# A linear-attention block with a GEGLU layer: regrouping the k^T v products, W_q's fold and the warming products

## The chip, the cores and the metric

The kernel runs on one core of a Trainium2 chip. The metric is the device time of one execution in microseconds (us); lower is better. Five engines work at once, each through its own list of instructions in order: TensorE (PE; its weight loads are shown apart as PEld) multiplies matrices and writes into PSUM, VectorE (DVE), ScalarE (ACT) and GpSimd (POOL) do elementwise work, and SyncE (SP) issues most DMA transfers. Semaphores make an instruction wait for another engine.

## What is computed

The input x has 2048 rows of 640. Attention has 32 heads of 20 columns, the feed-forward layer 1536 columns.

```python
def _A_ref(x, wqkv, w_phi, wo):          # H = 32, Dh = 20
    q, k, v = split(x @ wqkv)            # each [H, S, Dh]
    pq = einsum("bhsd,hdf->bhsf", q, w_phi)
    pk = einsum("bhsd,hdf->bhsf", k, w_phi)
    phi_q = concatenate([softmax(pq), softmax(-pq)], axis=-1)
    phi_k = concatenate([softmax(pk), softmax(-pk)], axis=-1)
    kv = einsum("bhsf,bhsd->bhfd", phi_k, v)
    z  = einsum("bhsf->bhf", phi_k)
    num = einsum("bhqf,bhfd->bhqd", phi_q, kv)
    den = einsum("bhqf,bhf->bhq", phi_q, z)[..., None] + 1e-6
    return merge_heads(num / den) @ wo
def _B_ref(x, w_gate, w_up, w_down):
    return (gelu(x @ w_gate) * (x @ w_up)) @ w_down
h = x + _A_ref(layernorm(x), wqkv, w_phi, wo)
return h + _B_ref(layernorm(h), w_gate, w_up, w_down)
```

The sum kv (and z) runs over all 2048 rows, so no row's attention can be finished before the last row's k and v are in it.

## The kernel before

The 2048 rows are 16 tiles of 128 rows (t = 0 to 15), four tiles to a block b. The 640 columns are five chunks of 128. The order of instructions on every engine is written out by hand: each engine runs its instructions in the order in which the program emits them.

PSUM has eight banks. Until the feed-forward part is well under way they are four buffers of two banks each (pool psG, tag "G"), which every matmul group takes in turn: a group waits until the engine that reads the buffer's former content is done.

**Opening (L187 to L230, L439 to L489).** SyncE issues the loads of x and of W_v, then transposing loads of W_k. TensorE meanwhile multiplies ones by ones (`warm`, L226 to L230; the result is never read): two products of 512 columns and 28 of 128, and four more of 128 at L447. The first real work are transposes of the first two tiles (L164) and the v products of tiles 0 to 2 (L312).

**Folding (`fold`, L232 to L259).** The per-head matrices w_phi are multiplied into W_k and W_q, so that one product with x gives pk or pq. For each of five row blocks d, TensorE multiplies the transposed weights by a block-diagonal matrix of w_phi (BD); the result wa fills two PSUM banks and is copied to bf16. Heads of 20 columns don't divide chunks of 128, so `runs` lists the pieces (bank, part, chunk, first and last column). W_k is folded with two parts of 320 columns, six products a block; W_q with `quarters` true in four parts of 160 columns, eight products a block, and the copy (L254 to L257, all on ScalarE) reorders the columns so that each 32-column piece of a head quarter lies in its place. W_q's folds run at t = 10 to 14 (L504).

**The loop over tiles (L494 to L534).** For each t: k's products (`k_tile`, L331) and exponentials, v's products for t + 3, softmax sums and normalization (`k_norm`, L343; VectorE and GpSimd). kv accumulates in one PSUM buffer kvp that stays taken from t = 3 on. `kv_tile` (L368) adds one row tile: 32 products of 32 x 40 outputs, four of them on different quarters of the array. They are issued in bursts: tiles 0 to 3 at t = 9 and 4 to 8 at t = 13 (`KVG`), tiles 9 to 12 at t = 15 behind the second group of q products (`KVQ`, L57 and L512), and tiles 13 to 15 behind the loop (L539).

**q (`q_mm`, `q_exp`, L387 to L401).** `QG` lists which (block, chunk) pairs form a group; a group has one or two, each of five products of 512 columns. Groups 0 to 3 run at t = 15; q = 4 is the first group behind the loop. After the exponentials of group 2 a one-element copy by GpSimd (L536) releases the load of W_gate.

**Attention's first tiles (L831 to L882).** `kv_mask` (L377) on VectorE scales kvp into KT and transposes it into KV. `attn_a` multiplies 40 small products (L585, tile ab) and copies them out; `attn_b`, `b2` and `b3` divide; `attn_t` transposes o; `attn_c` multiplies by W_o (L707). TensorE fills the time with the remaining q groups. Nine of the ten products of group q are issued ahead of `attn_a(0, 1)`, the tenth behind it (L831 to L834); `q_exp(q)` comes behind.

**The rest.** Gate and up products (L767), the down product (L789) and the attention of the remaining tiles are woven together by `weave`.

## Time and profile before

| | us |
|---|---|
| median of three runs | 271.77 |
| lowest and highest of them | 271.55, 272.08 |
| the profiled execution | 271.61 |
| its span, first to last instruction | 269.9 |

| engine | busy us |
|---|---|
| TensorE, products | 265.8 |
| TensorE, weight loads | 171.4 |
| VectorE | 174.9 |
| ScalarE | 138.9 |
| GpSimd | 101.0 |

The profile is taken from one execution. A row of a timeline has the start in us from the span's first instruction, the length, the engine, the line, the operation, what is written and read, its shape and how many were merged; in brackets stands how long the engine was idle before and what ended the idle time. A row of the chain has start, length and what the end of the kernel waited for at that moment. A matmul's recorded length includes its way through the array, so rows of neighbouring groups overlap; the chain cuts them where the next begins to count.

### The profile page before, as it was taken

To read this page: it belongs to the slowest core of one execution; us is meant where nothing else is said; L and a number is where in the kernel's file an instruction comes from. 1 tells how busy PE (TensorE), PEld (TensorE's weight loads), DVE (VectorE), ACT (ScalarE), POOL (GpSimd) and SP (SyncE) were. 2 spreads that over 40 slices of the span, in tenths; PEclk is the share of its full clock that TensorE was granted. 3 is DMA by queue.
4 is the path that set the end of the run, shared out by engine and by line. 5 is a ranking of instruction groups with operands and counts; after the bars stand their busy time and mean duration, and the time that the engine had idled before them with its cause. 6 is when DMAs were issued, how large, how long until landed. Compare 5 with 4: busy or idle time off the path is not lost.

```text
span 269.9 us, 7043 instructions
## 1 busy us (share of the span) xinstructions
PE 265.8 (98%) x2867; PEld 171.4 (64%) x2867; DVE 174.9 (65%) x347; ACT 138.9 (51%) x249; POOL 101.0 (37%) x238
## 2 busy tenths in 40 slices
PE   8999999999999999999999999999999999999995
PEld 6777777755456887788755555775555476444574
DVE  6889999997876858875576783568664322333322
ACT  5789998877789665245541456321554400322100
POOL 5548988796002335375211664014661100000000
PEclk9999999999999999999999999999999999999999
DMA  7989389310688343332202222203222101000011
GB/s 195 227 193 168 66 208 94 59 27 2 236 275 249 122 101 70 33 98 51 53 23 51 49 50 51 51 0 84 75 41 49 24 24 51 24 0 0 4 49 49
DMA packets 45264, 22.10 MB, mean 82 GB/s; under 512 B 37808, under 2 KB 43184, under 8 KB 45232
## 3 DMA queue, kind: packets, MB, share of 16 engines
q1 hardware_dynamic: 44576, 21.64, 33.6%
q8 instruction: 22, 0.36, 0.5%
q10 hardware_dynamic: 656, 0.03, 0.2%
q14 instruction: 10, 0.08, 0.1%
HBM read 10.18 MB, written 2.62 MB: 47 GB/s over the span
## 4 chain that ended last, share of the span: by engine, by line
PE 97%; DMA 2%; SPq 0%; DVE 0%; issue 0%
PE gu L767 39%; PE pd L789 20%; PE pq L396 8%; PE pk L296 8%; PE po L707 8%; PE pv L296 7%; PE kvp L374 2%; PE pv L312 2%; DMA Wv<-in_A_wqkv_dram 2%; PE ab L618 1%; PE wa L248 1%; PE ab L585 1%; PE tp L164 0%; SPq L193 0%; SPq L190 0%; SPq L189 0%
## 5 line engine op out<-in xcount | busy, mean ns | idle before, releaser
L770 ACT ACTIVATE g<-gu 128x512 bf16<-128x512 f32 (+1 forms) x60 | 30.4, 510 | 73.8 <-PE gu L767 73.0
L773 DVE TENSOR_TENSOR GT<-gu,g 128x512 bf16<-128x512 f32 (+1 forms) x60 | 34.4, 580 | 47.1 <-PE gu L767 39.2
L767 PE MATMUL gu<-LN2T,Wg 128*128 128x512 bf16 (+1 forms) x300 | 61.8, 337 | 0.0
L767 PE MATMUL gu<-LN2T,Wu 128*128 128x512 bf16 (+1 forms) x300 | 61.7, 336 | 0.0
L789 PE MATMUL pd<-Wd,GT 128*128 128x320 bf16 (+4 forms) x396 | 53.9, 295 | 0.0
L789 PEld LDWEIGHTS <-GT 128*128 128x128 bf16 x396 | 37.6, 98 | 14.5 <-DVE GT L773 0.2
L767 PEld LDWEIGHTS <-Wu 128*128 128x128 bf16 x300 | 29.3, 98 | 22.6
L767 PEld LDWEIGHTS <-Wg 128*128 128x128 bf16 x300 | 29.0, 98 | 21.2
L296 PEld LDWEIGHTS <-LN1T 128*128 128x128 bf16 x290 | 27.9, 98 | 10.5
L355 POOL TENSOR_TENSOR E<-E,rs 128x640 bf16<-128x640 bf16 x25 | 31.6, 1296 | 4.4 <-DVE rs L351 4.1
L791 DVE TENSOR_TENSOR y<-pd,x_sb 128x320 bf16<-128x320 f32 (+4 forms) x33 | 15.8, 480 | 23.8 <-PE pd L789 23.8
L707 PE MATMUL po<-Wo,oT 128*128 128x320 bf16 x160 | 24.5, 299 | 0.0
L296 PE MATMUL pk<-Wk,LN1T 128*128 128x320 bf16 x160 | 24.4, 299 | 0.0
L396 PE MATMUL pq<-LN1T,Wq 128*128 128x512 bf16 x100 | 22.9, 379 | 0.0
L347 DVE TENSOR_REDUCE sk<-E 128x64 f32<-128x1280 bf16 x16 | 22.9, 1430 | 0.0
L401 ACT ACTIVATE Eq<-pq 128x1024 bf16<-128x1024 f32 (+1 forms) x26 | 19.9, 831 | 2.8 <-PE pq L396 2.7
L340 ACT ACTIVATE E<-pk 128x640 bf16<-128x640 f32 x28 | 18.8, 747 | 3.0 <-PE pk L296 3.0
L707 PEld LDWEIGHTS <-oT 128*128 128x128 bf16 x160 | 15.6, 98 | 7.3 <-ACT oT L165 0.2
L296 PE MATMUL pv<-Wv,LN1T 128*128 128x320 bf16 x130 | 19.8, 299 | 0.0
L151 ACT ACTIVATE ln<-x_sb,v,rstd 128x640 bf16<-128x640 bf16 x14 | 12.9, 920 | 13.3 <-POOL v L746 13.2
L396 PEld LDWEIGHTS <-Wq 128*128 128x128 bf16 x100 | 9.4, 98 | 10.3
L682 DVE TENSOR_TENSOR tt<-AB,w 128x1280 bf16<-128x1280 f32 x10 | 15.1, 1506 | 0.4 <-POOL w L675 0.3
(120 smaller groups left out, 290.6 us busy)
## 6 DMA issues: line engine op xcount, KB each, us to landing
out_dram<-y SPq DMA_DIRECT2D x15, 160.0 KB, 1.8
x_sb<-in_A_x_dram SPq DMA_DIRECT2D x6, 320.0 KB, 3.4
Wu<-in_B_w_up_dram SPq DMA_DIRECT2D x1, 1920.0 KB, 8.9
Wg<-in_B_w_gate_dram SPq DMA_DIRECT2D x2, 768.0 KB, 5.6
Wd<-in_B_w_down_dram SPq DMA_DIRECT2D x1, 1440.0 KB, 6.7
Wo<-in_A_wo_dram SPq DMA_DIRECT2D x1, 800.0 KB, 5.1
x_sb<-in_A_x_dram SPq DMA_DIRECT2D x4, 160.0 KB, 2.8
Wv<-in_A_wqkv_dram SPq DMA_DIRECT2D x2, 320.0 KB, 4.3
```

The source lines that it names most:

```text
L296: nc.tensor.matmul(ps[:, u, 0:HD], lhsT=lnT(t, c), rhs=W[:, c, u * HD:(u + 1) * HD], start=(c == 0), stop=(c == NC - 1))
L340: nc.scalar.activation(Ek[t][:, s, :].rearrange("p (u f) -> p u f", u=2), pk[:, :, 0:HD], ACTF.Exp, scale=((lnp[t][2], nrstd[t]) if t in C ...
L347: nc.vector.reduce_sum(sk, Ek[t].rearrange("p s (h f) -> p (s h) f", f=Dh), axis=AX.X)
L355: eng.tensor_tensor(e, e, rs[:, s * H:(s + 1) * H, None].to_broadcast([P, H, Dh]), ALU.mult)
L396: nc.tensor.matmul(pqs[j][:, i, :], lhsT=Wq2[:, kc, c * P:(c + 1) * P], rhs=LN1T[b][:, kc, :], start=(kc == 0), stop=(kc == NC - 1))
L401: nc.scalar.activation(Eq[j][:, :, s, :], pqs[j][:, 0:len(QG[j])], ACTF.Exp, scale=(1.0, -1.0)[s])
L707: nc.tensor.matmul(pos[u], lhsT=st[t][:, c, :], rhs=Wo[:, c, u * HD:(u + 1) * HD], start=(c == 0), stop=(c == NC - 1))
L767: nc.tensor.matmul(gu[i][:, 0:n], lhsT=W[:, c, f * P:(f + 1) * P], rhs=LN2T[b][:, c, a0:a1], start=(c == 0), stop=(c == NC - 1))
L770: nc.scalar.activation(g[:, 0:n], gu[0][:, 0:n], ACTF.Gelu_apprx_tanh)
L773: nc.vector.tensor_tensor(st[b, "g", f][:, a0:a1], gu[1][:, 0:n], g[:, 0:n], ALU.mult)
L789: nc.tensor.matmul(pd[:, 0:f1 - f0], lhsT=st[b, "g", f][:, tl * P:(tl + 1) * P], rhs=Wd[:, f, f0:f1], start=(f == 0), stop=(f == NF - 1), ...
L791: nc.vector.tensor_tensor(y[:, f0:f1], pd[:, 0:f1 - f0], x_sb[b][:, tl, f0:f1], ALU.add)
```

## The change

```diff
@@ -54,7 +54,6 @@
     KVG = {9: (0, 1, 2, 3), 13: (4, 5, 6, 7, 8)}
-    KVQ = {1: (9, 10, 11, 12)}
     VC = Dh + 1
@@ -227,12 +226,12 @@
-    warm(*[512] * 2, *[P] * 28)
+    warm(*[512] * 8, *[P] * 4)
 
     def fold(WT, W2, quarters, ds=range(NC)):
 
 
-        n, w = (2, QF) if quarters else (1, HD)
+        n, w = 1, HD
         runs = []
@@ -251,8 +250,8 @@
             dst, src = W2[:, d, :].rearrange("p (u f) -> p u f", u=2), wr[:, :, 0:w]
             if quarters:
-                dst = W2[:, d, :].rearrange("p (c r f) -> p r c f", c=NC, r=4)
-                src = src.rearrange("p r (c f) -> p r c f", c=NC)
+                dst = W2[:, d, :].rearrange("p (c u m f) -> p u m c f", c=NC, u=2, m=2)
+                src = src.rearrange("p u (m c f) -> p u m c f", m=2, c=NC)
@@ -509,8 +508,6 @@
                 q_mm(j)
                 q_exp(j)
-                for i in KVQ.get(j, ()):
-                    kv_tile(i)
@@ -536,7 +533,7 @@
-    for t in range(13, NT):
+    for t in range(9, NT):
         kv_tile(t)
     kv_mask()
@@ -828,10 +825,8 @@
-    q_mm(q, (0,))
-    q_mm(q, (1,), (0, 1, 2, 3))
+    q_mm(q)
     attn_a(0, 1)
-    q_mm(q, (1,), (4,))
     q_exp(q)
```

The burst of tiles 9 to 12 between q's groups 1 and 2 goes, and its products are issued with those of tiles 13 to 15 behind group 3. All ten products of group q are issued ahead of `attn_a(0, 1)`. W_q's fold writes two halves of 320 columns, six products a block, and its copy takes one more dimension in its pattern. The first warming group has eight products of 512 columns and four of 128.

## The prediction

> **What bounds the kernel now.** I read the page first, then the chain of waits in order of time, then the timelines of single engines around the places that the change touches.

> ```profile
> span 269.9 us, 7043 instructions
> PE 265.8 (98%) x2867; PEld 171.4 (64%) x2867; DVE 174.9 (65%) x347; ACT 138.9 (51%) x249; POOL 101.0 (37%) x238
> ...
> PE 97%; DMA 2%; SPq 0%; DVE 0%; issue 0%
> ```

> TensorE is busy for 265.8 of 269.9 us and 97% of the chain runs through it; the 2% of DMA is the opening. So an edit counts by the TensorE time that it adds or takes away, or by a wait that it opens in that nearly closed stream. The change moves nothing to or from another engine. The chain through the place where three of its edits meet reads (start, length, what):

> ```profile
> 57.09 4.32 PE pq L396 x20
> 61.41 1.13 PE kvp L374 x128
> 62.54 3.34 PE pq L396 x15
> 65.89 0.87 PE kvp L374 x96
> 66.75 2.05 PE pq L396 x9
> 68.80 0.40 PE ab L585 x40
> 69.20 2.48 PE pq L396 x11
> 71.68 0.40 PE ab L585 x40
> 72.08 4.86 PE pq L396 x22
> 76.94 0.68 PE po L707 x5
> 77.62 0.28 PE tp L164 x5
> ```

> The pieces touch: each starts where the one before ends, so no wait of TensorE is left between 57.09 and 77.90 (77.62 + 0.28). A q product costs 4.32/20 = 0.216 us. After a burst of small products the next q group costs more than its products: 3.34 - 15 x 0.216 = 0.10 us, 2.05 - 9 x 0.216 = 0.11, 2.48 - 11 x 0.216 = 0.10. I call this 0.10 us the exit of a burst. Between the two bursts here 32 products make 1.13 - 0.87 = 0.26 us, 8.1 ns each, which leaves 0.87 - 96 x 0.0081 = 0.09 us as the entry.

> **Part 1, four bursts into three.** Removed: the burst of tiles 9 to 12 between the second and third block group of q. Added: the same 128 products in front of those of tiles 13 to 15, so one burst of 224. By the terms above it takes 0.09 + 224 x 0.0081 = 1.91 us, against 1.13 + 0.87 = 2.00, and one exit goes: 0.09 + 0.10 = 0.19 us less. The bursts before that are longer or run beside transfers give the other bound:

> ```profile
> 38.76 1.30 PE kvp L374 x128
> ...
> 52.37 1.56 PE kvp L374 x160
> ```

> ```profile
> 39.50:39.90 0.40, 0.40 (x51) 0.40 (x38) 1.00 1.12 214
> ...
> 61.50:62.30 0.80, 0.80 (x121) 0.80 (x109) 1.00 0.00 0
> 66.00:66.60 0.60, 0.60 (x96) 0.60 (x79) 1.00 0.00 0
> ```

> These bursts took 1.30 us for the same 128 products, and 1.56 for 160, which is 0.17 over 0.09 + 160 x 0.0081 = 1.39. The windows (length; busy and products of TensorE; busy and weight loads; clock, DMA share, GB/s) show the dip: 51 products touch 0.4 us with the DMA engines at 1.12, against 121 in 0.8 us and 96 in 0.6 with none. If the dip comes with length and not with DMA, the 224 could keep 1.30/128 = 10.2 ns throughout: 2.28 us, so the edit costs 2.28 - 2.00 - 0.10 = 0.18 us instead of saving 0.19. I take the saving, because the two bursts that are joined ran without any DMA; both ends go into the range.

> What the move lets go earlier, and whether the operands are ready:

> ```profile
> 62.09 3.38 DVE L355 TENSOR_TENSOR E<-E,rs 128x640 bf16<-128x640 bf16 x2
> 66.84 0.45 DVE L381 TENSOR_SCALAR KT<-kvp,sc,bi 128x160 bf16<-128x160 f32 x1 [1.37 <-PE kvp L374]
> ...
> 68.26 0.58 DVE L383 STREAM_TRANSPOSE KV<-KT 128x384 bf16<-128x384 bf16 x1
> ```

> The 35 q products now run in one piece, 57.09 + 35 x 0.216 = 64.65, and the burst runs from 64.65 to 66.56. Its last operand, VectorE's second normalization, is ready at 62.09 + 3.38 = 65.47; tile 15 is reached only after six tiles, 64.65 + 0.09 + 192 x 0.0081 = 66.30. This cover is 0.8 us; were it gone, all lateness beyond it would count. The third block group of q moves up from 62.54 to 61.41, so its exponentials and with them GpSimd's one-element copy that lets the W_gate transfer start move up too:

> ```profile
> 64.84 2.92 ACT L401 ACTIVATE Eq<-pq 128x1024 bf16<-128x1024 f32 x4 [1.46 <-PE pq L396]
> 69.32 0.75 ACT L652 COPY AB<-ab 128x704 f32<-128x704 f32 x1 [1.55 <-issue]
> 69.96 1.95 ACT L401 ACTIVATE Eq<-pq 128x1024 bf16<-128x1024 f32 x2
> ```

> ```profile
> 67.06 0.89 SPq L538 DMA_DIRECT2D Wg<-in_B_w_gate_dram  x2
> 73.74 1.21 SPq L167 DMA_TRANSPOSE oT<-o  x1
> ```

> ScalarE waited 1.46 us before 64.84, so it follows TensorE and starts about 1.1 us earlier; the two W_gate transfers are issued near 66.0 instead of 67.06. Nothing is queued behind them on SyncE until the transpose of o at 73.74, so nothing else moves. Price nothing.

> **Part 2, the q products around the first attention tile.** The tenth product of block pair q, 0.216 us, moves from behind the 40 ab products of tile 0 to in front of them. The sum of TensorE's work is the same and both groups keep their exit. What shifts is who is late. The ab products need VectorE's second transpose, done 68.26 + 0.58 = 68.84, which is 2.09 us after the burst; ten products plus exit are 2.26 us, so the cover grows from about 0 to 0.17. But the copies of ab and the exponentials of pair q behind them on ScalarE now start 0.216 us later against TensorE's stream. They end 69.96 + 1.95 = 71.91, which is 2.71 us after the ab products ended at 69.20. Pair q + 2 started 72.08, 2.88 us after that end; with one product less between it would start 2.66 after it. The code has four PSUM buffers of two banks; at that point pair q + 1 and the two ab halves of tile 1 hold three that ScalarE hasn't read yet, so q + 2 takes the one that pair q's exponentials free. It is late by 2.71 - 2.66 = 0.05, and with a hand-over like the 0.12 us from 69.20 to ScalarE's 69.32, by 0.17. The bounds are 0 (if ScalarE's order shifts with TensorE) and 0.17; I take 0.10, between the two. Behind the waiting product on TensorE stand pairs q + 2 to q + 4 and then po. On VectorE the chain of tile 1 ends with o:

> ```profile
> 76.39 0.49 DVE L686 TENSOR_TENSOR o<-tt 128x640 bf16<-128x640 bf16 x1
> ```

> It ends at 76.88 and TensorE transposes o at 77.62, a cover of 0.74 us of which the edits use 0.2 to 0.4. Price nothing.

> **Part 3, W_q's fold.** Five folds, each eight products into quarters, become six into halves; the products removed are two per block, with their weight loads, while the 720 columns stay (140, 100, 80 and 40 twice, against 140 four times and 80 twice). The fold of W_k has had the six-product shape:

> ```profile
> 11.16 0.98 PE wa L248 x18
> ...
> 13.50 0.32 PE wa L248 x6
> ```

> ```profile
> 42.89 0.33 PE wa L248 x8
> ```

> Six take 0.98/3 = 0.327 or 0.32 us, eight take 0.33: 0.003 to 0.01 less each, 0.02 to 0.05 for five; I take 0.03. The copy to bf16 on ScalarE keeps its 640 elements and 64-byte runs, with one more step in its pattern. [...]

> **Part 4, the opening's warming products.** Thirty (2 x 512 and 28 x 128 columns) become twelve (8 x 512 and 4 x 128). Both are 4,608 columns.

> ```profile
> 0.83 4.00 PE L228 MATMUL wu<-const-bfloat16-1.0 128*128 128x512 bf16 x30 [0.83 <-PEq L921]
> 4.92 0.89 PE L164 MATMUL tp<-ident,xc 128*128 128x128 bf16 x10
> 5.65 0.39 PE L228 MATMUL wu<-const-bfloat16-1.0 128*128 128x128 bf16 x4
> 6.36 0.30 PE L312 MATMUL pv<-Wv,LN1T 128*128 128x320 bf16 x1 [0.32 <-DMA Wv<-in_A_wqkv_dram]
> ```

> 4.00 us for 4,608 columns is 0.87 ns a column, so TensorE runs at half its later rate there (0.216 us for 512 is 0.42 ns). Twelve products end by 4.83 as well, before the transposes at 4.92; what comes next, pv at 6.36, waits for the DMA of W_v (0.32 us idle). Price nothing; if the cover were gone, every 0.1 us that the warming lasts past 4.92 + 0.32 would count.

> **Sum.** -0.19 + 0.10 - 0.03 + 0 = -0.12 us on the span of 269.9. Around the span lie 271.61 - 269.9 = 1.71 us, so the profiled execution would become 271.49. The profiled run is 0.16 below the median of the three runs, 271.77; a median over other runs is to be expected between 271.49 and 271.65, and I say 271.6.

> **Rivals.** (a) Products cost by number, not columns. Then part 3 saves 10 x 41 ns = 0.41 us, and with part 1 and no buffer wait 0.41 + 0.19 = 0.60: 271.61 - 0.60 = 271.0. For it: burst products of 40 columns cost 8.1 ns and no column count explains that. Against it: the W_k fold, six at the price of eight. [...]

> (b) Slower: TensorE's clock comes late in the opening. The four warming products at 5.65 last 0.39 us; at the early rate of 128 x 0.87 = 111 ns they would take 0.44 at least, so a faster rate was there by then, while the 4.00 us row says that it hadn't been for most of the time before 4.8. If the wide products leave the engine at half rate past 6.36, all pv products pay double. One more stretch as long as the 4.00 us would end near 9.6, 3.2 us past 6.36, and cost half of it, 1.6 us; I price the middle, 0.8: 271.49 + 0.8 = 272.3. It decides only if the turn comes 0.7 us later than now. Against it: equal columns, the same start, and no reason in the trace that 512-wide products count for less. [...]

> (c) The dip comes with length: +0.18 for part 1 instead of -0.19, and the buffer wait stays, 271.61 + 0.18 + 0.10 - 0.03 = 271.9; within what counts as no change.

> That the edits are all too small to be told apart from nothing is the forecast itself.

> **How the numbers follow.** Forecast 0.55, (a) 0.18, (b) 0.16, (c) 0.11. A difference of 0.2%, 0.54 us, is about what a measurement of this kernel can tell from no change (its three runs spread over 0.53). Faster takes (a) nearly whole and 0.03 of the forecast's runs: 0.20. Slower takes (b), a third of (c) and 0.03 of the forecast: 0.23. The rest, 0.57, is no change. The forecast alone, with the bounds of its terms (-0.19 to +0.18; 0 to 0.17; -0.05 to 0) and the spread of runs, spans 271.3 to 272.0; to leave out no more than 2 in 10 I reach to (a) and (b): 270.9 to 272.4.

> **What would show it.** Right: one kvp piece of 224 products of 1.9 to 2.0 us ending near 66.6; the ab products at 68.8 to 69.0; a wait of TensorE of about 0.1 us in front of pair q + 2, named after ScalarE; folds of 0.32 to 0.33 us; pv's first product at 6.36. Wrong: a burst over 2.1 us; folds near 0.25; pv products spaced over 0.2 us after 6.4, or any wait over 0.3 us in the chain where now the pieces touch.

## The result and the profile after

The changed kernel takes 273.46 us (median of six runs, 273.10 to 273.57) against 271.82 of the kernel before (six runs, 271.55 to 272.08): the ratio is 1.006 [1.0049, 1.007], or 1.6 us slower. The prediction was 271.6 with a range from 270.9 to 272.4. The profiled execution takes 273.36, 1.75 more than that of before.

The page of the changed kernel: span, busy time and count of instructions, and the queue that the profile names "instruction" (packets, MB, share of the DMA engines' time).

```profile
span 271.6 us, 6987 instructions
PE 266.4 (98%) x2839; PEld 170.4 (63%) x2839; DVE 175.0 (64%) x347; ACT 138.7 (51%) x249; POOL 100.8 (37%) x238
...
q8 instruction: 22, 0.36, 0.6%
```

TensorE's busy time grew by 0.6 us (265.8 to 266.4) and the span by 1.7, so most of the loss lies in places where TensorE stands. The waits of TensorE (what, for what, total us, times, longest) name three that were not there before:

```profile
PE po L704 <- DMA oT<-o: 0.5, 1, 0.5
PE ab L582 <- issue: 0.4, 1, 0.4
...
PE pk L295 <- ACT E L339: 0.2, 1, 0.2
```

"issue" means that the profile shows nothing that the instruction waited for. The chain of the changed kernel through the regrouped products, and then where po waits (its 3.45 us of "issue" are ScalarE's, ahead of the copy of ab, which follows the late ab products):

```profile
57.55 7.55 PE pq L395 x35
65.11 1.88 PE kvp L373 x218
66.98 3.45 issue
70.43 0.75 ACT AB L649
71.18 1.85 ACT Eq L400 x2
...
73.07 4.91 PE pq L395 x22
...
95.42 1.28 PE po L704 x10
96.70 4.36 DMA oT<-o
...
101.11 1.53 PE po L704 x10
102.64 2.18 PE gu L764 x20
```

and the same two points of the kernel before:

```profile
94.39 1.36 PE po L707 x10
...
100.88 2.18 PE gu L767 x20
```

Set beside the chain of before that the prediction shows, the lateness builds up in four steps:

| point | before | after | later by | step |
|---|---|---|---|---|
| first q product | 57.09 | 57.55 | 0.46 | opening, +0.46 |
| end of the last burst | 66.75 | 66.98 | 0.23 | one burst fewer, -0.23 |
| pair q + 2 | 72.08 | 73.07 | 0.99 | first attention tile, +0.76 |
| po of the third tile | 94.39 | 95.42 | 1.03 | |
| gate products behind the next po | 100.88 | 102.64 | 1.76 | transpose of o, +0.73 |

The rest runs as before. TensorE's timeline shows what the 0.76 is made of:

```profile
66.97 2.33 PE L395 MATMUL pq<-LN1T,Wq 128*128 128x512 bf16 x10
69.24 0.29 PE L582 MATMUL ab<-KV,Eq 32*128 32x44 bf16 x15
69.98 0.34 PE L582 MATMUL ab<-KV,Eq 32*128 32x66 bf16 x25 [0.45 <-issue]
70.25 2.33 PE L395 MATMUL pq<-LN1T,Wq 128*128 128x512 bf16 x10
72.52 0.47 PE L582 MATMUL ab<-KV,Eq 32*128 32x44 bf16 x40
```

TensorE stops for 0.45 us among the 40 products of one group. All that the forty read was ready: VectorE's second transpose into KV ended at 69.13 (its row stands under Part 2), and ScalarE's exponentials of the groups before at 66.99 (64.07 + 2.92):

```profile
64.07 2.92 ACT L400 ACTIVATE Eq<-pq 128x1024 bf16<-128x1024 f32 x4 [0.22 <-PE pq L395]
```

With what it takes to get going again, the next q product comes at 70.25 instead of 69.64 (69.24 + 0.40 for forty), 0.61 late. The other 0.15 stands in front of pair q + 2: the ab products count to 72.92 (72.52 + 0.40) and q starts at 73.07, when ScalarE's exponentials end (71.18 + 1.85 = 73.03).

The weight loads of the same place stop at the same point (x16, then a pause):

```profile
69.23 0.18 PEld L582 LDWEIGHTS <-Eq 32*128 32x128 bf16 x16 [0.42 <-issue]
69.98 0.23 PEld L582 LDWEIGHTS <-Eq 32*128 32x128 bf16 x24 [0.57 <-issue]
```

Products and loads both stop, with nothing awaited. That points at the instructions themselves. The q8 row has 22 packets, 0.36 MB, some 16 KB each; 2,839 products and as many loads over 22 packets make about 129 products a packet (the profile misses some products). That q8 carries TensorE's list is read from this count; the padded kernel below, with 102 products more, has 23 packets. The DMA activity of the changed kernel from 67.5 to 69 us, just ahead of the stop:

```profile
...
q8 instruction: 1, 0.02, 3.6%
```

### The profile page after: what moved, and what is told of

The parts are those of the page before. It is cut to its first block, busy times and chain, and to the rows that moved or that the text cites. A ratio compares the mean times of both kernels' runs of the same rounds, so it can differ in the third digit from the quotient of the medians.

```text
span 271.6 us, 6987 instructions
## 1 busy us (share of the span) xinstructions
PE 266.4 (98%) x2839; PEld 170.4 (63%) x2839; DVE 175.0 (64%) x347; ACT 138.7 (51%) x249; POOL 100.8 (37%) x238
## 4 chain that ended last, share of the span: by engine, by line
PE 87%; DMA 4%; DVE 2%; issue 2%; ACT 2%; SPq 1%; POOL 1%
PE gu L764 37%; PE pd L786 19%; PE po L704 8%; PE pq L395 6%; PE pk L295 6%; PE pv L295 5%; PE kvp L373 2%; DMA Wv<-in_A_wqkv_dram 2%; DMA oT<-o 2%; PE ab L615 1%; DMA x_sb<-in_A_x_dram 1%; DVE stats L120 1%; ACT Eq L400 1%; PE pv L311 1%; PE wa L247 1%
```

## The experiments

Beside F stood these rivals: a late semaphore or operand at the joined burst; the dip in the rate of long bursts, rival (c); the warming products' width and TensorE's clock, rival (b). The first four kernels were timed with one set of 17 runs of the kernel before (271.86), the others with another of 28 (271.76).

**One burst alone.** Fold, warming products and the split of group q stay as before.

```diff
-    KVQ = {1: (9, 10, 11, 12)}
-                for i in KVQ.get(j, ()):
-                    kv_tile(i)
-    for t in range(13, NT):
+    for t in range(9, NT):
```

> Theory F (instruction supply): TensorE's instructions come in packets of 16 KB, 256 instructions or 128 products; a packet is asked for when TensorE is some 320 instructions ahead of where the packet's first instruction stands, and is usable about 4.1 us later (the changed kernel's packet at 67.57 us and the gap that ends at 69.98). 320 instructions of small products run in 1.3 us. Here only the burst is merged, so every instruction in front of it stands 56 later in the list than in the changed kernel, and the request and the need of one packet both fall into the burst of 224: a stop of 4.1 - 1.3 = 2.8 us inside that burst, near its 222nd product, and a time of about 271.8 + 2.6 = 274.4 us, slower than the whole change. Rival D (the merged burst or what is behind it waits for data): the gap stays in the 40 ab products, at 0.4 to 0.5 us, and the time is no more than 272.7 us.

It took 274.95 (273.95 to 275.88), ratio 1.0123 [1.009, 1.0156]: the part that was to save 0.19 us costs 3.1 at the median when alone, and at least 2.1 in each of its four executions. TensorE's timeline of this kernel:

```profile
64.47 1.99 PE L373 MATMUL kvp<-E,vS 128*32 128x40 bf16 x222
68.89 0.20 PE L373 MATMUL kvp<-E,vS 128*32 128x40 bf16 x2 [2.43 <-issue]
...
73.94 0.47 PE L582 MATMUL ab<-KV,Eq 32*128 32x44 bf16 x40
74.34 3.84 PE L395 MATMUL pq<-LN1T,Wq 128*128 128x512 bf16 x16
```

A stop of 2.43 us with two of 224 products left, and VectorE had written the last operand long before:

```profile
61.91 3.38 DVE L354 TENSOR_TENSOR E<-E,rs 128x640 bf16<-128x640 bf16 x2
```

It ends at 65.29 (61.91 + 3.38), 1.2 us ahead of the stop. So neither an operand nor a dip in rate explains it: the 222 run at the rate of shorter bursts. What F says of the place: this kernel has 18 more warming products and 10 more fold products ahead than the changed one, so the same place of the list must come 28 products earlier. In the changed kernel it is product 224 + 10 + 16 = 250 from the burst's first (16 ab products by the weight loads), here 222, and 222 + 28 = 250. The 320 instructions and 4.1 us in the expectation are an estimate that fits the changed kernel: 69.98 - 4.1 = 65.88 us, when (65.88 - 65.11 - 0.09)/0.0081 = 84 products of its burst were done, 250 - 84 = 166 products or 332 instructions ahead of the stop. No run shows the two separately; the stop of 2.8 us made from them was 2.43.

**Fold and warming alone**, the bursts as before.

```diff
-    warm(*[512] * 2, *[P] * 28)
+    warm(*[512] * 8, *[P] * 4)
-        n, w = (2, QF) if quarters else (1, HD)
+        n, w = 1, HD
...
```

> Only W_q's fold and the warming products are changed; the bursts are those of before. Theory F: no stop around the bursts, since between a packet's request and its need lie 30 or more q products (over 6 us with the bursts); the stage from the last burst to group q + 2 takes 5.3 us as before; but the list behind the loop has the changed kernel's numbering, so the instruction packet that met the transposing transfer of o at 96.7 us in the changed kernel meets it again: that transfer takes over 4 us and TensorE waits 0.5 us for it. Time 272.2 to 272.6. Rival D: 271.7, the folds saving 0.06, no wait for the transfer. Rival O (the opening: fewer warming products delay W_v or the clock): W_v lands near 6.7 us instead of 6.3 and the whole kernel is 0.4 us later from there on: 272.2, seen in the opening.

272.52 (272.18 to 273.43), ratio 1.0026 [1.0013, 1.0039]. The profiled execution is the slowest of the eight, 273.43, so its waits are larger than those of the median. No stop by "issue" is left, but the wait for the transpose of o is there, as are late v and k products in the opening:

```profile
PE po L707 <- DMA oT<-o: 0.5, 1, 0.5
PE pk L296 <- ACT E L340: 0.3, 1, 0.3
PE pv L296 <- DMA LN1T<-ln: 0.2, 1, 0.2
```

So the two losses outside the joined burst come with this half of the change, the stop with the other half.

**The changed kernel with thirty warming products again**: 18 products more in the list, no other difference.

```diff
-    warm(*[512] * 8, *[P] * 4)
+    warm(*[512] * 2, *[P] * 28)
```

> The changed kernel with the warming products of before (30 instead of 12), which puts every later instruction 36 further in the list and changes nothing else behind the opening. Theory F: the stop moves 18 products up, out of the 40 ab products into the ten q products in front of them, and is 0.9 to 1.1 us long instead of 0.45; the ab products then run without a gap. Time 273.5 to 274.0, unless the transfer of o at 96.7 us is no longer met by a packet (then 0.5 less). Rival D: the gap stays where it was, at the seventeenth ab product, 0.45 us. Rival O: W_v lands near 6.3 us again and the time falls by 0.4 us.

272.58 (271.79 to 272.95), ratio 1.0021 [1.0009, 1.0032]. The stop has moved out of ab into the q products; TensorE's timeline:

```profile
64.64 2.00 PE L373 MATMUL kvp<-E,vS 128*32 128x40 bf16 x224
66.57 1.90 PE L395 MATMUL pq<-LN1T,Wq 128*128 128x512 bf16 x7
69.13 0.60 PE L395 MATMUL pq<-LN1T,Wq 128*128 128x512 bf16 x2 [0.66 <-issue]
```

F puts it at 250 - 18 = 232, which is 224 + 8. The rows show 7 + 2 of ten q products, so one record is missing; the weight loads settle that eight stand ahead of the stop:

```profile
66.57 1.41 PEld L395 LDWEIGHTS <-Wq 128*128 128x128 bf16 x8
```

The sizes fit as well: if the lead is a fixed number of products, each of the 8 q products in it lasts 0.216 instead of 0.008 us, and with the 0.10 of the burst's exit the stop must be 1.77 us shorter than the 2.43 where all of the lead is burst. Measured: 0.66, which is 1.77 less. For the changed kernel (ten q products, 16 of ab) the same gives 0.2; measured 0.45. What had been expected, a stop of 0.9 to 1.1 us and 273.0 us or more, was too much; the place was right.

**The changed kernel with 102 more products in the list**, narrow ones in the opening.

```diff
-    def warm(*cols):
+    def warm(*cols, m=P):
-            nc.tensor.matmul(wu[:, 0, 0:n], lhsT=ones[:, 0:P], ...)
+            nc.tensor.matmul(wu[0:m, 0, 0:n], lhsT=ones[:, 0:m], ...)
-    warm(*[512] * 8, *[P] * 4)
+    warm(*[512] * 2)
+    warm(*[32] * 112, m=32)
```

> The changed kernel with 114 warming products (2 of 512 columns, 112 of 32 columns and 32 weight columns) instead of 12, about the same time in the opening, and 204 more instructions in the list. Theory F: the request then falls 385 instructions into the burst's list and the need lies behind both groups of ten q products; the stop is 0 to 0.3 us, the ab products run without a gap, and the stage from the start of q's first group to group q + 2 is at least 0.4 us shorter than in the changed kernel; more instructions make it faster: 271.6 to 272.4. Rival D: nothing changes behind the opening, 273.4, or slower by what the additional products cost.

280.19 (277.79 to 280.44), ratio 1.0285 [1.024, 1.0329]: a miss in time by 8 us. The places of the two stops are those of F; TensorE's timeline:

```profile
66.72 1.37 PE L374 MATMUL kvp<-E,vS 128*32 128x40 bf16 x148
68.99 0.77 PE L374 MATMUL kvp<-E,vS 128*32 128x40 bf16 x76 [0.91 <-issue]
69.70 2.33 PE L396 MATMUL pq<-LN1T,Wq 128*128 128x512 bf16 x9
71.96 0.47 PE L583 MATMUL ab<-KV,Eq 32*128 32x44 bf16 x40
72.36 0.39 PE L396 MATMUL pq<-LN1T,Wq 128*128 128x512 bf16 x1
75.59 3.04 PE L396 MATMUL pq<-LN1T,Wq 128*128 128x512 bf16 x8 [2.84 <-issue]
```

148 + 102 = 250 again. The second stop comes 76 + 10 + 40 + 2 = 128 products on (so the weight loads; two records of q products are missing), one packet later. I had expected the packet border to be covered by q products at both places. They didn't cover: the second packet, recorded at 72.91, came while the load of W_gate filled the DMA engines (a share of 1.08 in the window from 72 to 73 us), and before the stop was over TensorE's clock fell. Windows of this kernel (length; busy us and instructions of PE, PEld, DVE, ACT, POOL; clock; DMA share; GB/s):

```profile
74.00:74.50 0.50, 0.00 (x0) 0.00 (x0) 0.43 (x3) 0.50 (x2) 0.00 (x0) 0.99 0.04 6
74.50:75.00 0.50, 0.00 (x0) 0.00 (x0) 0.47 (x3) 0.50 (x1) 0.00 (x0) 0.50 0.05 18
...
77.00:78.00 1.00, 1.00 (x4) 0.33 (x3) 0.00 (x0) 0.00 (x0) 0.00 (x0) 0.55 0.00 0
```

Two of the four executions kept a mean clock of 1.0 and still took 280.30 and 277.79, so the loss doesn't need the clock. Another part was lost in the opening, where the third piece of W_v came late; the first q product counts from 59.23, 2.1 us later than before:

```profile
10.04 2.60 PE L312 MATMUL pv<-Wv,LN1T 128*128 128x320 bf16 x18 [1.09 <-DMA Wv<-in_A_wqkv_dram]
```

**The place, counted from the start.** The stops can also be placed without F's sums. The weight loads recorded from the start of the span up to a moment inside each stop (in a row of windows the figure with x behind PEld's busy time, here x989), for the changed kernel:

```profile
0.00:69.70 69.70, 68.21 (x988) 46.95 (x989) 61.92 (x112) 55.97 (x88) 49.26 (x96) 1.00 0.61 130
```

| stop | weight loads ahead of it | record of the packet starts | next product or load |
|---|---|---|---|
| changed kernel | 989 | 67.57 | 69.98 |
| one burst alone | 989 | 66.18 | 68.89 |
| thirty warming products again | 989 | 66.41 | 69.12 |
| padded, first stop | 989 | 66.36 | 68.99 |
| padded, second stop | 1,117 | 72.91 | 75.22 |

The work at this place differs (ab products, the burst, q products, the burst), but the place in the list is the same, and the second stop is 128 further on. From the start of a packet's record to the next work it is 2.3 to 2.7 us each time. W_gate's transfer was under way at all five stops; no run shows what they would be without it.

**Warming products alone, by width and by number.** The first kernel has the change's eight wide and four narrow, the rest as before. The second keeps them wide (seven of 512) and restores the number, 30, with 19 of 32 columns (`warm` with the argument m of the padded kernel).

```diff
-    warm(*[512] * 2, *[P] * 28)
+    warm(*[512] * 8, *[P] * 4)
```

> Only the warming products are changed: 12 instead of 30, so every later instruction stands 36 earlier in TensorE's list. Theory F: no stop at the bursts. The instruction packet that came at 94.8 us before comes about 18 products later, near 97 us, inside the transposing transfer of o issued at 95.7; that one takes over 4 us instead of 2.8 and TensorE waits 0.3 to 0.5 us. If the opening depends on the numbering or the width of the warming products, q's first group starts 0.3 us or more later than 56.9 us. Time 272.1 to 272.6. Rival N (all that is seen in the opening is scatter of the loads): 271.8 to 272.2.

```diff
-    warm(*[512] * 2, *[P] * 28)
+    warm(*[512] * 7, *[P] * 4)
+    warm(*[32] * 19, m=32)
```

> The kernel before with wide warming products but as many of them: 7 of 512, 4 of 128 and 19 of 32 columns with 32 weight columns, 30 in all, so the numbering of TensorE's list is that of before. If the count is what matters (theory F): no stop, no late transfer, 271.8, q's first group at 56.9. If the width matters (rival O): W_v lands 0.2 to 0.4 us later and q's first group starts at 57.3 or later: 272.2.

Twelve products: 272.46 (271.89 to 272.91), ratio 1.0021 [1.001, 1.0033]. Thirty with wide ones among them: 271.85 (271.47 to 272.52), ratio 1.0005 [0.9995, 1.0015]. The columns are nearly the same (4,608 and 4,704); with the number the loss goes. So it isn't the width. The first twelve v products take 1.79 us in both kernels, as in the one before and the changed one, so the v products ran at the same rate with wide and with narrow warming products, which removes rival (b). The profiled execution of the twelve, 271.89, is the fastest of its ten and shows little of the loss: q's first product counts from 57.28, against 57.30 with the equal number, and po starts without a wait.

**The fold alone.**

```diff
-        n, w = (2, QF) if quarters else (1, HD)
+        n, w = 1, HD
...
```

> Only W_q's fold is changed, six products a block: 20 instructions fewer behind t = 14, none in the opening. Both theories: five folds of 0.32 instead of 0.33 us, no stop at the bursts, opening as before. Theory F: the packet of 94.8 us moves about 10 products later, to about 96 us, in front of the transfer's data; no wait. Time 271.7 to 271.9.

271.60 (271.27 to 272.33), ratio 0.9992 [0.9979, 1.0004]: no difference that can be told. It is the fastest kernel of this study, but not shown to be faster than the one before; the interval reaches down to 0.57 us less.

**The changed kernel once more**, one execution on that chip.

> The changed kernel once more, for a second profile. Theory F: the gap of 0.4 to 0.6 us stands again behind the sixteenth ab product of tile 0, and the transfer of o near 96.7 us takes over 4 us again. If the late opening is of the change, q's first group starts again near 57.4 us; if it is scatter of the loads, W_v lands anywhere from 6.3 to 6.7 us. Time 273.1 to 273.6.

272.94, where 273.1 to 273.6 with a stop of 0.4 to 0.6 us had been expected. The stop has all but gone; TensorE's timeline of this execution:

```profile
69.59 0.53 PE L582 MATMUL ab<-KV,Eq 32*128 32x44 bf16 x40
...
72.32 0.47 PE L582 MATMUL ab<-KV,Eq 32*128 32x44 bf16 x40
72.87 3.40 PE L395 MATMUL pq<-LN1T,Wq 128*128 128x512 bf16 x15
```

Forty ab products take 0.53 us instead of 0.47, again with a pause of some 0.1 us behind load 989: the packet, recorded at 67.30, came almost in time. The stop of the changed kernel varies from run to run; the wait of 0.15 in front of pair q + 2 (72.32 + 0.40 to 72.87) and the losses of the other half stay: po waits 0.3 us, and q's first product counts from 57.91.

**The transpose of o.** This is the transfer that is issued near 96 us (98.36 in the padded kernel). The changed kernel from 98.7 to 99.2 us, and the kernel before over its whole transfer, which has no q8 row (last line: issues and us to landing):

```profile
...
q8 instruction: 1, 0.02, 13.3%
```

```profile
oT<-o SPq DMA_TRANSPOSE x1, 2.8
```

Where a q8 packet falls inside the transfer it takes 4.36 (changed kernel), 4.32 (fold and warming), 4.13 (changed kernel once more), 3.74 (warming alone) and 3.48 us (padded). Where the packet comes earlier it takes 2.8 (before) and 2.59 to 2.64 us (one burst, thirty warming products again, equal number, fold alone). Of the first sort four have twelve warming products, all five of the second thirty. That the packet is the difference, and not something else that goes with twelve, shows in the transfer that follows: it is issued at 103.75 us in the kernel before and at 103.78 with the fold alone, both with thirty. In the first a packet starts 1.79 us behind the issue, in the second none before the landing:

```profile
q8 instruction: 1, 0.02, 1.5%
...
oT<-o SPq DMA_TRANSPOSE x1, 4.1
```

```profile
oT<-o SPq DMA_TRANSPOSE x1, 2.5
```

The ten traces hold 129 transposes of o behind 70 us. The 17 in which a q8 packet starts 0.5 to 2.2 us behind the issue take 3.13 to 4.37 us, three with a packet right behind the issue (up to 0.23 us) 2.55 to 2.83, and the 109 without 2.36 to 3.24.

In the opening it is alike: from 12 to 13 us one q8 packet comes in each kernel with thirty warming products and none in those with twelve, where it comes later, at 13.24 to 14.67 us. The transposing load issued at 12.8 to 13.1 us (LN1T, L166 or L167) takes 3.01 to 3.33 us in the five with thirty and 3.77 to 4.25 in the four with twelve; in two of these four, fold and warming and the changed kernel once more, the v products wait 0.2 us for it.

## Why the prediction was wrong

**The step that failed** is the end of Part 1, "so nothing else moves. Price nothing", and with it the "Price nothing" of Part 4. Both priced what the moved and removed products do on TensorE, and which transfers SyncE issues. Neither asked how TensorE's own instructions arrive. The q8 row stood on the page of before, with 22 packets, and the count of products (2,867) beside it. By it 224 products in 1.9 us are nearly two packets. The runs showed in its place stops of 0.06 to 2.84 us at fixed places of TensorE's list, where the next packet of instructions is late, and transposing transfers longer by 0.7 to 1.6 us than the 2.8 of before where a packet falls into them. In the changed kernel the terms put at nothing came to 0.46 us in the opening, 0.61 at the stop and 0.73 behind the transpose of o. None of the three rivals had this cause; what the prediction named as a sign of its error, a wait over 0.3 us where the pieces touched, came twice: 0.45 us at ab and 0.5 at po.

**Part 1, the burst.** The size of the burst was right: predicted 1.91 us, 1.88 in the chain, and the step of joining saved 0.23 (predicted 0.19). So rival (c), the dip with length, is out. The stop behind it was the miss: 0.06 to 0.45 us in two executions of the changed kernel, 0.66 with 18 more products, 2.43 with 28 more. In the kernel before the same list place, 222 from e1's burst start, falls on the 94th product of its last burst (20 + 128 + 15 + 94 = 35 + 222 = 257 from the first q product); the fifteen q products between the bursts add 15 x 0.208 = 3.1 us to the lead, more than the 2.43 that was missing. So the split into two bursts had been covering the packet. With a lead between 106 products (94 and the 12 q products that make up 2.43) and 222, and if the lead is a fixed number, the time from asking to use is an estimated 2.43 + 106 x 0.0081 = 3.3 to 2.43 + 222 x 0.0081 = 4.2 us.

**Part 2, pair q + 2.** Right: 0.15 to 0.16 us in three executions with the ten products together (the padded kernel, stopped just before, has none), within 0 to 0.17 (0.10 taken), behind ScalarE's exponentials. In the kernel with the burst alone, which keeps the split, the ab products count to 74.34 (73.94 + 0.40), where q starts: no wait. The cover of 0.17 us for the ab products held as well; the KV transpose ended at 69.13 (68.55 + 0.58), before 69.24.

```profile
68.55 0.58 DVE L382 STREAM_TRANSPOSE KV<-KT 128x384 bf16<-128x384 bf16 x1
```

**Part 3, the fold.** Right: six products take 0.32 us, and alone it changes nothing that can be told. Rival (a), cost by number at 41 ns a product (0.33/8 in the fold of before), is out by this row: two products fewer at 41 ns would make 0.25. The time alone doesn't exclude its 0.41 us.

```profile
43.43 0.32 PE wa L247 x6
```

**Part 4, the warming products.** No real product came later by the warming products themselves; pv's first came at 6.74 rather than 6.36 since W_v landed later (6.70, below). But twelve instead of thirty move every packet border 18 products later in the work (the stop came 250 products from the burst's first in the changed kernel and 232 with thirty), and that costs 0.7 us at the median (272.46 - 271.76). In the profiles of the three other executions with twelve it shows as two things: the transpose of o, 1.3 to 1.6 us longer than the 2.8 of before with a cover of about 1 us, leaves a wait of 0.3 to 0.5; and a late opening, by 0.46 to 1.12 us at the first q product (57.55, 57.91 and 58.21 against 57.09). In the profiled execution of warming alone the transfer was 0.9 longer and was covered; where its median execution loses 0.7 no trace shows.

**What stays open.** Of the 0.46 us that the changed kernel lost before its first q product, W_v's landing (4.52 us against 4.14 before, on its chain) may be one part; that landing scattered between kernels of equal opening too. It isn't needed for a late opening: in the changed kernel once more W_v landed at 6.41, 0.1 us later than before, and the first q product came 0.82 us later. How the 0.46 us divide between this scatter and the later packet isn't settled. Why a packet lengthens a transposing transfer isn't known; that it does, the comparison above shows. The padded kernel's second stop is larger than the fixed lead gives; its packet's delay under the load of W_gate is the likely cause, not a separately tested one.

## What to carry to other kernels

Count the instructions as well as their time: here TensorE stood for 2.43 us behind a run of 222 very short products (1.99 us), and 15 products of 0.2 us between such runs are what covered the next packet. An edit that only changes a count early in the list, even of products nobody waits for, moved later packets here (the one of 12 to 13 us with thirty warming products came at 13.24 to 14.67 with twelve), so a change of this kind is judged by experiments that keep the count. An idle time put down to "issue" in the middle of a group of equal products, with the weight loads stopped too, was the sign; the next stop of the padded kernel stood 128 products further on (989 and 1,117 loads), which is where to look.

## What the runs showed of the hardware

The packets of 16 KB move little (0.6% of the DMA engines' time for all 22 in the changed kernel), yet TensorE stood for up to 2.84 us (padded kernel) at a place where one was late, and transposes of o with a packet 0.5 to 2.2 us behind their issue took 3.1 to 4.4 us instead of 2.4 to 3.2. TensorE's granted clock was 0.50 in the padded kernel's profile from about 74.5 us, while its 2.84 us stop lasted, to 77.9 (0.55 in the window from 77 to 78), and 1.00 from 78: about 3.4 us (77.9 - 74.5) of low clock. In the kernel with the burst alone, two of four executions showed a mean clock of 0.994 and took 275.88 and 275.59 us, the two at 1.0 took 273.95 and 274.31, 1.3 to 1.9 us less. A mean of 0.994 is what 3.4 us at half clock, as in the padded kernel's profile, would make of 274 us (3.4 x 0.5 / 274 = 0.006); this is an estimate, since no trace of the two slower executions shows where their clock fell. The profiled execution had the stop of 2.43 us at a mean clock of 1.0.
